# Attention and a squared-ReLU layer on one core: transposes moved from VectorE and TensorE to DMA, with a new order of all engines

## The chip, the cores and the metric

The kernel runs on one core of one Trainium2 chip. Its time is the device time of one execution in microseconds; the time before is 251.46 us, the median of three runs (251.16 to 253.64). The engines of the core run side by side, each through its own queue in order: TensorE (PE in the profile), VectorE (DVE), ScalarE (ACT), GpSimd (POOL) and SyncE (SP). SP only issues DMAs. POOL issues the DMAs that change float32 to bfloat16 under way.

## What is computed

Eight batches of eight heads, 576 tokens, 64 values a head; 32 packing queries a head. Two attentions, then one dense layer with a squared ReLU, on 4608 tokens:

```python
def _attn_ref(q, k, v, p):
    scale = 1.0 / np.sqrt(q.shape[-1])
    def sm_attn(qq, kk, vv):
        s = scale * np.matmul(qq, kk.transpose(0, 1, 3, 2))
        s = s - np.max(s, axis=-1, keepdims=True)
        a = np.exp(s)
        a = a / (np.sum(a, axis=-1, keepdims=True) + 1e-09)
        return np.matmul(a, vv)
    p_packed = sm_attn(p, k, v)
    return sm_attn(q, p_packed, p_packed)

def _moe_ref(x, w_in, w_out):
    r = np.maximum(x @ w_in, 0.0)
    return (r * r) @ w_out
```

`w_in` is 512x2048, `w_out` 2048x512. Inputs and output are float32.

## The kernel before

Work is tiled in quads: four heads of one batch, so two quads a batch, 16 in all. A quad is named by batch and quad, so `s121` is the step `s1` of batch 2, quad 1. The steps of a quad are these.

- `Lk`, `Lq`, `Lv` load keys, queries and values by POOL's queue as bfloat16 (288 KB each), into three buffers for each of the three.
- `kT`, `qT` turn keys and queries in 32x32 blocks on VectorE (lines 279 and 285).
- `s1` (line 295) are the packing queries' scores: 16 TensorE matmuls of 32 rows, 32 columns and 288 moving columns, into PSUM. From batch 2 on both quads run together, with quad 1's heads swapped in pairs (`group`, `PAIRED`), so that eight of these matmuls can lie side by side in the array instead of four.
- `m1`, `x1`, `rd`: row maximum on VectorE, exponential on ScalarE with the sum beside it, reciprocal.
- `eT`, `eo`: six TensorE transposes of the softmax `e1` into PSUM and their copy to SBUF by ScalarE or VectorE.
- `pv` (24 small matmuls) and `pp` (times the reciprocal): the packed values.
- `bd` turns them in 32x32 blocks for the second scores; `pt`, `po` turn them on TensorE and copy them out for `wp`.
- `s2`: scores of the queries, like `s1`; `t2` turns the scores on VectorE (line 383).
- `m2`, `sb`, `x2`, `su`, `a2`, `aT`: the second softmax, and its turn in 32x32 blocks, on VectorE, ScalarE and GpSimd.
- `w0`, `w1` and `W0`, `W1`: the packed values times `w_in` (`wp`, line 422), and copies out of PSUM.

The dense layer follows. `hB.H.F` (`h0.F` in batch 0) makes the hidden block F of batch B, half H: two quads' `wp` times `a2T`, matmuls of 128x128 by 288 columns (line 438). `r` is the ReLU out of PSUM, on ScalarE or VectorE, `q` the square into `gT` on VectorE (line 479). `oT.j` are two of the 16 matmuls of output tile T (line 490), `c` copies the tile out of PSUM and issues its two output DMAs on SP's queue (line 510). There are 36 output tiles and three `o_sb` buffers. `Z` words are idle matmuls on zeros. `Wi`, `Wo`, `Pr`, `P0`, `P1`, `Pt` load and prepare the weights and the packing queries.

Nothing is scheduled by a compiler: the string `ORDER` holds one word for each step, a suffix names the engine (`:v` VectorE, `:a` ScalarE, `:p` GpSimd), and every engine takes its instructions in the order of the words. Waits follow from the tiles that are read and written. An engine whose next instruction waits holds everything behind it.

Of the kernel before, what the change touches and what calls it, by code (L numbers as in the profile page):

```python
# [21 lines left out]
D = 64  # L22
# [9 lines left out]
PAIRED = range(2, 8)  # L32
# [21 lines left out]
o3.5 po20:a bd21 h1.0.12 h1.0.3 w020 q1.0.2 o3.6 r1.0.12:a r1.0.3:a h1.0.7 h1.0.13 q1.0.0 Lk30 qT20 o3.7 W020:a bd20
o4.0 r1.0.13:a c3:a r1.0.7:v q1.0.1 h1.0.10 q1.0.6 h1.0.11 q1.0.3 s22 r1.0.10:a h1.0.8 r1.0.11:a r1.0.8:a h1.0.9
Lq30 o4.1 t220 h1.0.14 r1.0.9:a o4.2 t221 q1.0.4 r1.0.14:a h1.1.0 r1.1.0:a pt21 h1.0.15 m221 o4.3 po21:a h1.1.2
r1.0.15:a w021 w120 q1.0.5 h1.1.10 o5.0 sb21:v r1.1.2:a W021:a o4.4 h1.1.8 m220 x221 Lv31 r1.1.10:a sb20:v o5.1 Lk31
r1.1.8:a x220 o4.5 h1.1.3 r1.1.3:a h1.1.11 o4.6 r1.1.11:a kT30 W120:a h1.1.4 kT31 r1.1.4:a w121 q1.0.7 h1.1.1 o5.2
o4.7 r1.1.1:a h1.1.6 o5.3 su20 W121:a su21 Lq40 h1.1.5 r1.1.5:a r1.1.6:v c4:a o5.4 s13 a221:v h1.1.7 q1.1.0 r1.1.7:a
h1.1.14 q1.1.5 o5.5 r1.1.14:a h1.1.15 r1.1.15:a a220:v Lk40 o5.6 aT21 o5.7 q1.1.1 q1.1.2 h1.1.12 q1.1.3 Lk41 aT20  # L60
c5:a h1.1.13 Lq31 r1.1.12:a o6.0 o6.1 h1.1.9 r1.1.13:a r1.1.9:a o6.2 Lv41 m131 h2.0.2 q1.1.4 r2.0.2:a h2.0.3 o6.3
m130 h2.0.0 r2.0.3:a o6.4 h2.0.4 kT40 q1.1.7 r2.0.0:a x130 o7.0 h2.0.8 r2.0.4:a o6.5 Lv30 r2.0.8:a eT30 x131 h2.0.6
rd30 o7.1 eo30:v h2.0.7 o7.2 eT31 r2.0.6:a q1.1.6 o6.6 o6.7 qT30 r2.0.7:a rd31 qT31 q2.0.1 h2.0.1 h2.0.14 pv30
eo31:a r2.0.1:a pv31 o7.3 pp31:a c6:a r2.0.14:v h2.0.5 q2.0.0 o7.4 h2.0.10 pp30:a r2.0.5:v o7.5 bd30 r2.0.10:a
h2.0.12 pt30 r2.0.12:a o7.6 h2.0.9 h2.0.11 po30:a kT41 w030 bd31 w130 r2.0.11:a W030:a r2.0.9:v q2.0.3 h2.1.6 q2.0.2
r2.1.6:a h2.0.13 o7.7 r2.0.13:a o8.0 W130:v c7:a h2.0.15 h2.1.7 r2.0.15:a s23 q2.0.4 h2.1.0 r2.1.7:v q2.0.7 o8.1
r2.1.0:a h2.1.14 t230 o8.2 t231 h2.1.12 r2.1.14:a Lq41 q2.0.6 m231 o8.3 o8.4 Lv40 r2.1.12:a pt31 q2.0.5 h2.1.1 o8.5
o9.0 h2.1.15 r2.1.1:a h2.1.4 r2.1.4:a o8.6 r2.1.15:a o9.1 o8.7 m230 h2.1.10 po31:v sb31:v o9.2 h2.1.13 x231 o9.3
o9.4 r2.1.10:a sb30:v su31 r2.1.13:a h2.1.8 q2.1.3 c8:a w131 w031 q2.1.0 h2.1.11 o9.5 x230 r2.1.8:v r2.1.11:a a231:v
W031:a q2.1.6 h2.1.2 o9.6 r2.1.2:v h2.1.5 su30 o9.7 a230:v q2.1.7 h2.1.3 aT31 W131:a r2.1.5:a o10.0 o10.1 o10.2 s14  # L70
h2.1.9 aT30 c9:a r2.1.3:a o10.3 q2.1.1 h3.0.8 o10.4 o10.5 r2.1.9:a r3.0.8:a h3.0.2 h3.0.0 m140 q2.1.4 x140 m141
r3.0.2:a x141 q2.1.2 q2.1.5 o11.0 eT40 eo40:v h3.0.6 o11.1 r3.0.0:a rd41 o11.2 h3.0.3 eT41 r3.0.6:a h3.0.1 qT40 qT41
r3.0.3:a o10.6 Lk50 eo41:a r3.0.1:v h3.0.7 o10.7 rd40 q3.0.1 pv40 pv41 r3.0.7:a pp40:v q3.0.0 h3.0.4 h3.0.5 pt40
o11.3 r3.0.4:a h3.0.9 c10:v Lk51 o11.4 r3.0.5:v r3.0.9:a q3.0.4 o11.5 h3.0.10 o11.6 po40:a pp41:a h3.0.12 pt41 bd40
r3.0.10:a q3.0.3 h3.0.14 r3.0.14:v r3.0.12:a o11.7 h3.0.15 bd41 w140 po41:a q3.0.2 w040 r3.0.15:v h3.1.2 W040:a
o12.0 W140:a o12.1 r3.1.2:v h3.0.11 o12.2 o12.3 kT51 q3.0.7 r3.0.11:v h3.1.0 kT50 s24 h3.1.4 r3.1.0:v c11:a o12.4
t241 o12.5 r3.1.4:a o12.6 h3.1.5 o12.7 r3.1.5:a h3.0.13 q3.0.5 r3.0.13:a o13.0 h3.1.6 o13.1 m241 c12:a sb41:v h3.1.3
r3.1.6:a r3.1.3:a x241 t240 o13.2 h3.1.1 r3.1.1:a o13.3 h3.1.7 o13.4 o13.5 r3.1.7:a q3.0.6 Lv51 m240 sb40:v h3.1.8
Lq51 w141 w041 q3.1.2 o13.6 o14.0 r3.1.8:a x240 h3.1.9 su41 o13.7 o14.1 Lv50 h3.1.14 W041:a c13:a a241:v r3.1.9:v
r3.1.14:a h3.1.15 o14.2 su40 W141:a o14.3 q3.1.1 h3.1.12 o14.4 r3.1.15:a s15 aT41 h3.1.10 o14.5 Lv61 a240:v o14.6  # L80
r3.1.12:a q3.1.0 h3.1.13 r3.1.10:a aT40 q3.1.4 m150 m151 h4.0.2 r3.1.13:a o15.0 o15.1 h4.0.10 r4.0.2:a o14.7 q3.1.6
q3.1.3 o15.2 x150 h4.0.4 r4.0.10:a o15.3 h3.1.11 c14:v r4.0.4:v x151 eT50 eo50:a q3.1.7 eT51 h4.0.8 r3.1.11:v q3.1.5
o15.4 h4.0.5 Lk61 r4.0.8:v o15.5 eo51:v h4.0.12 Lk60 r4.0.5:v pv50 pv51 h4.0.9 rd51 r4.0.12:a o16.0 h4.0.11 Lq50
r4.0.9:a q4.0.4 rd50 o16.1 r4.0.11:a pp50:v pp51:a h4.0.3 o16.2 pt51 qT50 o15.6 h4.0.0 po51:v r4.0.3:a r4.0.0:a
q4.0.5 o15.7 Lq60 h4.0.14 pt50 c15:a q4.0.1 h4.0.1 o16.3 r4.0.14:a o16.4 po50:v r4.0.1:v h4.0.15 h4.1.0 w050 q4.0.2
w150 bd51 r4.1.0:a r4.0.15:a o16.5 h4.0.6 kT60 q4.0.0 h4.1.1 r4.1.1:a q4.0.7 o16.6 bd50 r4.0.6:v o17.0 h4.1.2 Lk71
W050:a h4.1.3 r4.1.2:a W150:v o17.1 o17.2 qT51 r4.1.3:a h4.0.13 kT61 r4.0.13:a h4.0.7 q4.0.6 s25 h4.1.6 t251
r4.0.7:a t250 o16.7 q4.1.0 o17.3 o17.4 o17.5 c16:a m250 r4.1.6:a h4.1.10 h4.1.4 r4.1.4:a o17.6 sb50:v w151 w051
r4.1.10:a h4.1.5 h4.1.11 o17.7 m251 o18.0 r4.1.5:a h4.1.8 r4.1.11:a o18.1 Lq71 q4.0.3 qT60 c17:a h4.1.9 Lk70 o18.2
q4.1.2 o18.3 o18.4 o18.5 r4.1.8:a sb51:v W051:a o18.6 o19.0 x250 r4.1.9:a x251 W151:a h4.1.12 h4.1.7 q4.1.1 o18.7  # L90
c18:a o19.1 r4.1.12:a Lq61 su50 s16 a250:v o19.2 su51 a251:v m160 h4.1.14 r4.1.7:a o19.3 h4.1.13 o19.4 aT50
r4.1.14:a x160 o19.5 aT51 q4.1.3 m161 Lv60 h4.1.15 o19.6 r4.1.13:a h5.0.10 o20.0 r4.1.15:a h5.0.2 x161 q4.1.5 q4.1.4
o19.7 r5.0.2:a o20.1 eT61 r5.0.10:v h5.0.6 h5.0.3 eT60 c19:v r5.0.6:a o20.2 r5.0.3:v eo60:a q4.1.6 h5.0.4 eo61:v
r5.0.4:a h5.0.7 o20.3 q5.0.1 rd61 pv60 r5.0.7:a rd60 pp60:v pv61 h5.0.0 q4.1.7 Lv70 h5.0.11 o20.4 pt60 r5.0.0:a
h5.0.1 o20.5 r5.0.11:v pp61:a h5.0.5 o21.0 r5.0.1:a o20.6 po60:a h5.0.8 r5.0.5:a h5.1.2 qT61 kT71 q5.0.5 w160 q5.0.3
bd60 w060 q5.0.2 r5.0.8:a r5.1.2:a W060:a o21.1 h5.0.9 kT70 o21.2 W160:a r5.0.9:v bd61 Lv71 o20.7 o21.3 h5.1.3
q5.0.0 r5.1.3:v h5.0.14 s26 t260 h5.0.15 c20:a r5.0.14:a h5.0.12 r5.0.15:a r5.0.12:a o21.4 h5.1.0 o21.5 r5.1.0:a
q5.1.1 t261 h5.1.12 r5.1.12:a h5.1.1 o22.0 q5.0.4 r5.1.1:a h5.0.13 m260 o22.1 r5.0.13:v o21.6 h5.1.4 pt61 r5.1.4:a
sb60:v po61:a h5.1.13 o21.7 r5.1.13:a h5.1.6 o22.2 m261 q5.0.7 h5.1.14 x260 r5.1.6:a o22.3 r5.1.14:a o22.4 c21:a
sb61:v h5.1.5 h5.1.7 r5.1.5:a r5.1.7:a o22.5 su60 w061 q5.1.6 w161 q5.0.6 h5.1.15 h5.1.8 Lq70 x261 a260:v r5.1.15:a  # L100
q5.1.0 q5.1.2 aT60 o22.6 W061:a o22.7 o23.0 h5.1.10 r5.1.10:v o23.1 o23.2 r5.1.8:a h5.1.11 o23.3 c22:a o23.4 W161:a
su61 h5.1.9 q5.1.3 s17 o23.5 r5.1.11:a o24.0 a261:v aT61 o23.6 m170 h6.0.6 m171 r5.1.9:a o24.1 h6.0.2 o23.7 x170
# [525 lines left out]
```

## Time and profile before

| | |
|---|---|
| median of three runs | 251.46 us (251.16 to 253.64) |
| span of the profiled execution, first to last instruction | 248.6 us (its own time is not given beside the span) |
| first hidden matmul starts | 23.15 us |
| first output matmul starts | 37.28 us |
| last output matmul ends | 243.84 us |
| granted TensorE clock, mean | 0.995 |
| TensorE's share of the chain that ended last | 81% |
| cast loads: 288 KB, issue to landing, median | 7.2 to 8.1 us |
| output DMA: 128 KB, issue to landing, median | 2.8 us |

The span counts from the first to the last instruction of the core. Matmuls are pipelined: the duration of one in the groups is its latency, and what a step costs TensorE is read from the starts in the timeline. The chain of waits is followed back from the last instruction to whatever released it. The DMA share counts packets in flight on 16 engines and can exceed 1.

### The profile page before, as it was taken

To read this page: it belongs to the slowest core of one execution; us is meant where nothing else is said; L and a number is where in the kernel's file an instruction comes from. 1 tells how busy PE (TensorE), PEld (TensorE's weight loads), DVE (VectorE), ACT (ScalarE), POOL (GpSimd) and SP (SyncE) were. 2 spreads that over 40 slices of the span, in tenths; PEclk is the share of its full clock that TensorE was granted. 3 is DMA by queue.
4 is the path that set the end of the run, shared out by engine and by line. 5 is a ranking of instruction groups with operands and counts; after the bars stand their busy time and mean duration, and the time that the engine had idled before them with its cause. 6 is when DMAs were issued, how large, how long until landed. Compare 5 with 4: busy or idle time off the path is not lost.

```text
span 248.6 us, 6041 instructions
## 1 busy us (share of the span) xinstructions
PE 237.1 (95%) x2415; PEld 132.2 (53%) x2447; DVE 194.2 (78%) x411; ACT 145.7 (59%) x316; POOL 45.8 (18%) x75
## 2 busy tenths in 40 slices
PE   8998899998999999999999999999999999999992
PEld 5655554465556554655456555655555555555540
DVE  1888899978988899979887998898897798644710
ACT  2346784476968748755764658676957555353100
POOL 8329634350401500033000230010000000000000
PEclk9999999999999999999999999999999999999997
DMA  6999999999791992269812794252121213211323
GB/s 112 203 207 205 206 197 209 197 142 259 161 171 64 157 211 45 46 93 187 185 42 45 135 130 122 64 90 56 42 45 42 45 42 82 49 42 44 70 63 82
DMA packets 23358, 28.52 MB, mean 115 GB/s; under 512 B 4257, under 2 KB 14753, under 8 KB 23329
## 3 DMA queue, kind: packets, MB, share of 16 engines
q0 software_dynamic: 16880, 18.55, 47.1%
q1 hardware_dynamic: 6288, 9.44, 15.0%
q8 instruction: 19, 0.31, 0.5%
q10 hardware_dynamic: 160, 0.13, 0.2%
q14 instruction: 11, 0.08, 0.1%
HBM read 37.22 MB, written 9.44 MB: 188 GB/s over the span
## 4 chain that ended last, share of the span: by engine, by line
PE 81%; DMA 10%; issue 2%; DVE 2%; POOL 2%; ACT 1%; SPq 0%; ACTq 0%; POOLq 0%
PE ps_o L490 48%; PE ps_h L438 24%; DMA v_b<-in_v_dram 4%; PE ps_wp L422 3%; PE ps_s L295 3%; DMA w_in_bf<-in_moe_w_in_dram 3%; DMA out_dram<-o_sb 3%; PE ps_e1T L339 1%; PE ps_pv L352 1%; POOL k_b L242 1%; DVE mx L387 1%; POOL d L391 0%; ACT r L444 0%; POOL q_b L242 0%; PE ps_ppT L372 0%
## 5 line engine op out<-in xcount | busy, mean ns | idle before, releaser
L490 PE MATMUL ps_o<-w_out_bf,gT 128*128 128x512 bf16 x544 | 144.2, 379 | 2.0 <-issue 0.5
L444 ACT ACTIVATE r<-ps_h 128x288 bf16<-128x288 f32 (+1 forms) x181 | 73.1, 426 | 55.9 <-PE ps_h L438 47.5
L438 PE MATMUL ps_h<-a2T,wp 128*128 128x288 bf16 x512 | 91.9, 286 | 1.4 <-ACT r L444 1.4
L490 PEld LDWEIGHTS <-gT 128*128 128x128 bf16 x576 | 54.9, 98 | 42.1 <-issue 3.3
L438 PEld LDWEIGHTS <-wp 128*128 128x128 bf16 x512 | 47.4, 98 | 44.4 <-issue 7.7
L479 DVE TENSOR_TENSOR gT<-r 128x576 bf16<-128x576 bf16 x128 | 54.7, 448 | 5.2 <-ACT r L444 4.9
L446 DVE TENSOR_SCALAR r<-ps_h 128x288 bf16<-128x288 f32 (+1 forms) x59 | 28.5, 484 | 20.0 <-PE ps_h L438 18.8
L332 ACT CAST wp<-ps_wp 128x1024 bf16<-128x1024 f32 x29 | 28.9, 1016 | 3.8 <-PE ps_wp L422 3.7
L332 ACT COPY o_sb<-ps_o 128x512 f32<-128x512 f32 x27 | 15.9, 588 | 10.8 <-PE ps_o L490 9.4
L321 ACT ACTIVATE e<-ps_s,nm 128x576 bf16<-128x576 f32 x16 | 11.8, 736 | 13.0 <-DVE nm L316 13.0
L233 POOL DMA_DIRECT2D v_b<-in_v_dram x16 | 11.1, 695 | 44.2 <-PE ps_pv L352 22.5
L279 DVE STREAM_TRANSPOSE kT<-k_b 128x576 uint32<-128x576 uint32 x16 | 15.0, 943 | 5.1 <-DMA k_b<-in_k_dram 5.1
L263 PE MATMUL ps_idle<-nought 128*128 128x288 bf16 x95 | 14.4, 304 | 1.1 <-DVE nought L178 1.1
L383 DVE STREAM_TRANSPOSE s<-ps_s 128x576 f32<-128x576 f32 x16 | 12.0, 767 | 2.4 <-PE ps_s L295 2.4
L401 DVE TENSOR_REDUCE sums<-e 128x18 f32<-128x576 f32 x16 | 11.9, 741 | 1.4 <-ACT e L396 1.3
L242 POOL DMA_DIRECT2D k_b<-in_k_dram x16 | 9.0, 562 | 21.4 <-DVE kT L279 12.5
L422 PE MATMUL ps_wp<-w_in_bf,ppT 64*32 64x512 bf16 x256 | 11.4, 382 | 0.8 <-DMA w_in_bf<-in_moe_w_in_dram 0.7
L316 DVE TENSOR_REDUCE nm<-ps_s 128x1 f32<-128x576 f32 x16 | 11.6, 739 | 0.6 <-PE ps_s L295 0.6
L285 DVE STREAM_TRANSPOSE qT<-q_b 128x576 uint32<-128x576 uint32 x16 | 12.0, 761 | 0.0
L387 DVE TENSOR_REDUCE mx<-s 128x18 f32<-128x576 f32 x16 | 11.9, 743 | 0.1
L396 ACT ACTIVATE e<-d 128x576 f32<-128x576 f32 x16 | 11.0, 685 | 1.6 <-DVE d L391 1.4
L263 PEld LDWEIGHTS <-nought 128*128 128x128 bf16 x95 | 9.2, 103 | 4.9 <-issue 1.2
(47 smaller groups left out, 153.0 us busy)
## 6 DMA issues: line engine op xcount, KB each, us to landing
out_dram<-o_sb SPq DMA_DIRECT2D x70, 128.0 KB, 2.8
k_b<-in_k_dram POOLq DMA_DIRECT2D x16, 288.0 KB, 8.1
v_b<-in_v_dram POOLq DMA_DIRECT2D x16, 288.0 KB, 7.4
q_b<-in_q_dram POOLq DMA_DIRECT2D x10, 288.0 KB, 7.2
w_in_bf<-in_moe_w_in_dram POOLq DMA_DIRECT2D x4, 512.0 KB, 12.5
w_out_bf<-in_moe_w_out_dram POOLq DMA_DIRECT2D x4, 512.0 KB, 13.8
q_b<-in_q_dram POOLq DMA_DIRECT2D x12, 144.0 KB, 3.9
p_b<-in_p_dram POOLq DMA_DIRECT2D x1, 192.0 KB, 11.5
```

Of the source, the lines that this page charges most:

```text
L263: self.nc.tensor.matmul(ps[:, :HALF], lhsT=self.nought[:, :P], rhs=self.nought, start=True, stop=True)
L279: return self.nc.vector.transpose(t["kT"][:].rearrange("p (j l a) e -> p a j l e", j=J, a=3).bitcast(U32).rearrange("p a j l e -> p a j (l ...
L285: return self.nc.vector.transpose(t["qT"][:].rearrange("p s e -> p (s e)").bitcast(U32), t["q"][:].rearrange("p t d -> p (t d)").bitcast(U32))
L332: engine.copy(out, x)
L383: nc.vector.transpose(s2[:].rearrange("p (a t) i -> p a (t i)", a=2), t["ps_s2"][:, :, :HALF])
L387: self.nc.vector.tensor_reduce(out=t["mx"], in_=t["s2"], op=ALU.max, axis=AX.X)
L422: self.nc.tensor.matmul(ps[NP * h:NP * h + NP, c, :], lhsT=t["ppT"][D * c:D * c + D, NP * g:NP * g + NP], rhs=self.w_in_bf[D * c:D * c + D ...
L438: self.nc.tensor.matmul(ps, lhsT=t["wp"][:, fb // n, fb % n * P:(fb % n + 1) * P], rhs=t["a2T"][:, hf * HALF:(hf + 1) * HALF], start=(qd = ...
L444: engine.activation(r, ps, ACT.Relu)
L446: engine.tensor_scalar_max(r, ps, 0.0)
L479: (engine or self.nc.vector).tensor_tensor(out=out, in0=r, in1=r, op=ALU.mult)
L490: self.nc.tensor.matmul(self.o[tt], lhsT=self.gT[:, fb, a:a + P], rhs=self.w_out_bf[:, fb, :], start=(i == 0), stop=(i == self.NFB - 1))
```

## The change

- From batch 2 on, `kT`, `qT`, `eT`, `pt` are single DMA transposes, issued on SP's queue: 9 blocks of 128x128 for keys, 9 for queries, 6 for `e1`, one for the packed values. A sixth word, `Px`, turns a batch's packing queries (two blocks). The copies `eo` and `po` of these batches are gone.
- In batches 0 and 1 keys and queries are turned by nine TensorE transposes each (`kP`, `qP`) into PSUM and copied out (`kE`, `qE`); `eT` and `pt` stay on TensorE.
- A turned tile now has the 64 values of a head on 64 partitions, even and odd tokens in the two halves, so `s1` is 8 matmuls of 64 rows (from 16 of 32 rows), and so is `s2` from batch 2 on. In batches 0 and 1 `s2` is 72 matmuls of 32 moving columns that give the scores already turned; these have no `t2`. `bd`, `group` and `PAIRED` are gone.
- The keys of batch 0 are loaded as float32 on SP's queue, into space of `gT`, and cast by ScalarE and VectorE (`ka`, `kb`). The packing queries come on ScalarE's queue.
- `e1` lies in two fixed tiles with padded columns that are zeroed at the start.
- `c` is split: the copy stays `c`, the two output DMAs become a word `d`.
- Squares name an engine: 79 on VectorE, 49 on GpSimd. ReLUs are 131 on ScalarE and 109 on VectorE (181 and 59 before); output copies 14 and 21, besides the last tile's (27 and 8 before); subtractions on GpSimd 7 (3 before), multiplications 6 (3).
- All words stand in a new order; there are 59 idle matmuls for 95.

The core of the diff, with the order of the start and of batch 2's and the start of batch 3's attention:

```diff
-PAIRED = range(2, 8)
+TURNED = range(2, 8)
...
+Lk00 I Lk01 Lv01 Lq01 Pd:v Lq00 PT Lv00 PE:v kb00:a ka00:v Wi01 Z9 kP00 Wi00 kb01:v ka01:a Lk11 kE00:a Z5 kP01 Wi11
+kE01:v s100 Wi10 m100 Z2 s101 m101 x100 Lk10 x101 Z9 eT00 rd00 qP01 eo00:v eT01 rd01 Lq10 qE01:a qP00 eo01:v qE00:v
+pv01 pp01:a pv00 Wo2 pt01 pp00:v po01:a pt00 s201 po00:v s200 m201 m200 Lv11 sb01:v sb00:v x201 x200 su01 Z22 w000 Wo0
+w001 W000:a su00 a201:p W001:a a200:v Z6 kP11 Lv10 aT01 kE11:a aT00 Z6 h0.1 h0.11 r0.1:v Pr s111 r0.11:a m111 h0.10
...
+r1.0.4:v o5.0 r1.1.11:a o4.1 rd20 h1.0.5 eT20 h1.1.10 r1.0.5:v o5.1 r1.1.10:a h1.1.4 q1.0.2:v q1.1.5:p h1.1.3 kT31
+r1.1.4:v o4.2 r1.1.3:a pv21 q1.1.1:v Lq41 h1.0.13 pp21:a h1.0.12 r1.0.13:v o5.2 Px4 Lv30 r1.0.12:a h1.1.8 pt21
+q1.0.6:v h1.0.14 r1.1.8:a r1.0.14:v h1.0.6 pv20 r1.0.6:v h1.0.7 pp20:a Lv41 h1.1.9 r1.0.7:v pt20 s221 r1.1.9:a w021
+q1.0.3:v h1.0.15 q1.1.4:p W021:a t221 h1.1.5 kT30 o5.3 r1.1.5:v o4.3 r1.0.15:a m221 Lk40 w121 s220 q1.0.7:p q1.1.2:v
...
-        self.sm = pool("sm", 2)
+        self.sm = pool("sm", 4)
...
+        nc.scalar.dma_start(self.p_f, self.packed(0, G))
...
+        self.e1s = [self.consts.tile([P, J, P], BF16, name=f"e1x{i}") for i in range(2)]
+        for x in self.e1s:
+            nc.vector.memset(x[:, :, PS:], 0.0)
...
+    def p_x(self, b):
+        self.pX[b] = self.tp.tile([P, self.NQ, P], BF16, name="pX")
+        g = (b - TURNED[0]) * self.NQ
+        self.nc.sync.dma_start_transpose(self.pX[b], self.p_d[:, g:g + self.NQ].rearrange("p g e d -> p (g e d)"))
...
+            if (n, b) == ("k", 0):
+
+                f = self.gT[:, self.NFB - 1 - qd, :].bitcast(F32).rearrange("p (t d) -> p t d", d=D)
+                self.nc.sync.dma_start(f, s)
+                self.att.setdefault((b, qd), {})["f"] = f
...
+    def st_turned(self, t, n):
+        x = t[n + "T"] = self.tp.tile([P, T // 2, P], BF16, name=n + "T")
+        self.nc.sync.dma_start_transpose(x, t[n][:].rearrange("p t d -> p (t d)"))
...
+    def st_turn(self, t, n):
+        ps = t["ps_" + n] = self.turn16("ps_" + n)[:].rearrange("p a c -> p (a c)")[:, :T * D]
+        x = t[n][:].rearrange("p t d -> p (t d)")
+        for i in range(T // 2):
+            self.nc.tensor.transpose(ps[:, i * P:(i + 1) * P], x[:, i * P:(i + 1) * P], self.ident)
+
+    def st_turn_out(self, t, n, engine):
+        t[n + "T"] = self.tp.tile([P, T // 2, P], BF16, name=n + "T")
+        self.copy(engine, t[n + "T"][:].rearrange("p t c -> p (t c)"), t["ps_" + n])
+
+    def st_s1(self, t, b, qd):
+
+        ps = t["ps_s1"] = self.turn32("ps_s1")
+        for h in range(QH):
+            c = slice(NP * h, NP * h + NP)
             for e in range(2):
...
+                r = slice(D * e, D * e + D)
+                self.nc.tensor.matmul(ps[c, e, :HALF].rearrange("p (b a l) -> p a b l", a=3, b=3),
+                                      lhsT=self.pX[b][r, qd, c],
+                                      rhs=t["kT"][r, :, c].rearrange("p (a b) l -> p a b l", a=3), start=True, stop=True)
...
+        if b in TURNED:
+            for h in range(QH):
+                c = slice(NP * h, NP * h + NP)
+                for e in range(2):
+                    r = slice(D * e, D * e + D)
+                    self.nc.tensor.matmul(ps[c, e, :HALF], lhsT=t["ppT"][r, c], rhs=t["qT"][r, :, c], start=True, stop=True)
+            return
+
+        for i in range(T // 2):
+            for e in range(2):
+                for h in range(QH):
+                    r, c = slice(D * e, D * e + D), slice(NP * h, NP * h + NP)
+                    self.nc.tensor.matmul(ps[c, e, i * NP:(i + 1) * NP], lhsT=t["qT"][r, i, c], rhs=t["ppT"][r, c],
+                                          start=True, stop=True)
...
     def st_e1T(self, t, b):
+        if b in TURNED:
+            t["e1T"] = self.tp.tile([P, J, P], BF16, name="e1T")
+            self.nc.sync.dma_start_transpose(t["e1T"], t["e1"][:].rearrange("p j s -> p (j s)"))
+            return
...
     def st_ppT(self, t, b):
+        if b in TURNED:
+            t["ppT"] = self.keep.tile([P, P], BF16, name="ppT")
+            self.nc.sync.dma_start_transpose(t["ppT"][:].unsqueeze(1), t["pp"][:].rearrange("p e d -> p (e d)"))
+            return
...
+    def step_d(self, engine, tt):
+        nc, o = self.nc, self.o_sb.pop(tt)
```

## The prediction

> **What bounds the kernel now.** I read the busy table and the forty slices first, then the stages, then the costliest groups, then the landing times of the queue that the change loads.
>
> ```profile
> PE 237.1 (95%) x2415; PEld 132.2 (53%) x2447; DVE 194.2 (78%) x411; ACT 145.7 (59%) x316; POOL 45.8 (18%) x75
> ...
> DMA  6999999999791992269812794252121213211323
> ```
>
> TensorE is busy in nearly the whole span, and the DMA engines are full for the first quarter and half empty later. The stages (busy us of PE, PEld, DVE, ACT, POOL, then clock, DMA share, GB/s) say where an engine other than TensorE can matter:
>
> ```profile
> 0.00:23.10 23.10, 20.51 (x275) 13.06 (x275) 15.30 (x31) 9.76 (x16) 12.82 (x23) 1.00 1.07 180
> 23.10:37.30 14.20, 12.96 (x188) 7.81 (x185) 12.11 (x27) 10.83 (x18) 7.99 (x13) 1.00 1.34 202
> 37.30:60.00 22.70, 21.64 (x244) 10.91 (x245) 20.47 (x41) 12.69 (x26) 8.21 (x12) 1.00 1.13 199
> 60.00:120.00 60.00, 59.37 (x618) 33.34 (x627) 52.77 (x112) 43.17 (x100) 11.59 (x20) 1.00 0.71 133
> 120.00:180.00 60.00, 59.37 (x622) 32.89 (x630) 52.05 (x111) 40.92 (x93) 5.24 (x9) 1.00 0.46 87
> ```
>
> From 60 us on TensorE idles 1%, with VectorE at 87%: work taken off VectorE there gains little by itself, work taken off TensorE counts in full. The timeline gives the price of each TensorE step, start to start, where the groups give single latencies only:
>
> ```profile
> 51.53 0.83 PE L339 MATMUL ps_e1T<-ident,e 128*96 128x128 bf16 x12
> 52.20 0.59 PE L490 MATMUL ps_o<-w_out_bf,gT 128*128 128x512 bf16 x2
> 52.63 0.65 PE L438 MATMUL ps_h<-a2T,wp 128*128 128x288 bf16 x4
> 53.21 0.56 PE L352 MATMUL ps_pv<-v_b,e1T 96*32 96x64 bf16 x48
> 53.70 0.67 PE L438 MATMUL ps_h<-a2T,wp 128*128 128x288 bf16 x4
> ```
>
> So 12 transposes of `e1` take 0.67 us (0.335 a quad, 56 ns each), two output matmuls 0.43 (0.216 each), two pv steps 0.49. The same view gives 4 hidden matmuls 0.49 (0.122 each), a wp step alone 0.35 and two together 0.56: 0.216 a step (8 matmuls at once) and 0.13 for each run of small tiles among full ones. Likewise 0.62 for a score step alone (33.18 to 33.80; 4 at once) and for a pair (57.99; 8 at once): 4 x 0.122 + 0.13. A ppT transpose takes 0.06.
>
> From the first hidden matmul (23.15 us) to the end of the last output matmul (243.84) are 220.7 us. Work in it: 576 output matmuls 124.2, 512 hidden 62.6; batches 2 to 7 at 1.23 scores + 0.67 eT + 0.12 pt + 0.34 pv + 0.86 wp + some three further change-overs = 3.64 each, 21.8; batch 1 by the same prices 3.4, batch 0's last wp 0.7. Sum 212.8 (rounded), so 7.9 us are stalls. Before 23.15 lies a chain of loads and single small steps, with 95 idle matmuls as filler. Behind the last matmul lie 4.8 us, whose code stays the same.
>
> **TensorE's work, part by part.** In batches 2 to 7 the score steps become 8 matmuls of 64 rows, all on different parts of the array as in wp: 0.122 a quad and 0.13 where the run is new. Four score steps cost 0.49 for 0.98 of columns, but stand mostly alone, as wp now does too. eT (0.67) and pt (0.12) leave TensorE. Counted through the order with these prices a batch costs 2.45 instead of 3.64; six batches gain 7.1 us.
>
> Batch 1 pays: one kP and two qP of 9 transposes (0.5 each), two s1 and one more eT that now stand behind the first hidden matmul, and two s2 of 72 matmuls of 32 columns for 0.62 each before. The trace has no such form; pv's 48 in 0.49 (10 ns each) give 0.7, the paired scores' 32 in 0.62 (19 ns) 1.4. I take 1.1, the middle. Batch 1 comes to 6.9 for 3.4. The stretch holds 124.2 + 62.6 + 14.7 + 6.9 + 0.7 = 209.1: 3.7 us less.
>
> **The start.** `k00` and `k01` come as floats on SP's queue, 576 KB written each where a cast load wrote 288, beside POOL's four loads. Best case: issue at 0.74 and 2.2 to landing as `p_f`, plus 1152 KB at the page's best slice (259 GB/s): 7.3 us. Worst: half of the 207 GB/s: 12.4. I take 9.5 for `k01`: `k00` largely alone, as POOL's loads begin after the identity, `k01` at half rate. Then casts, 9 transposes and an eviction of 128x1152 from PSUM (1.0 by the 128x1024 cast): 2.4 to the scores; from there max 0.76, exp 0.74, transposes and eviction 1.0, pv, pp, pt, po 1.2, two s2 2.2, semaphores 0.6: 6.5; then the order fills Z22, two wp, Z6, kP11, Z6, 5.2 us, about the length of max, subtract, exp, sums, multiply and turn. First hidden matmul: 9.5 + 2.4 + 6.5 + 5.2 = 23.6, half a microsecond later than now (21.4 to 26.5 by the bounds). The idle matmuls, `I`, `Pd`, PT and the zeroing of the padding lie under these loads at no cost; without that cover they are 1 to 2 us. `w_in` comes by the same POOL queue behind one load less and is not last.
>
> **VectorE, ScalarE, GpSimd.** VectorE loses 15.0 (kT), 12.0 (qT), 3.1 (ppd), four turns of scores 3.1, 49 squares 20.9, and some 9 of subtracts, multiplies and evictions; it takes 50 more ReLUs (22.7), 13 output copies (9.0), five wp copies (6.1), three evictions (2.3): 171 for 194. ScalarE falls to about 107. GpSimd takes 49 squares; nearest row is its 128x576 multiply, 1.16 us (lower bound VectorE's 0.43), so 57 us, and seven more element-wise steps 8: 111 us of work. A square that lands late holds only the output matmuls that read that block; loads queue behind it on POOL. In this order a load of `v` stands 0.5 to 1.5 us of TensorE work behind the pv step that frees its buffer. I set these at no cost while the six `r` buffers cover a square, and take 2 of the 7.9 us of stalls off for the freer VectorE and ScalarE, since 2.3 us of TensorE's idle time lies between 23.1 and 60 where VectorE is at 85 to 90% (bounds 0 and 4).
>
> **SP's queue.** It carries, for a batch, 18 + 18 + 12 + 2 + 2 blocks of 128x128 (keys, queries, softmaxes, ppT, p), 312 in all, 10.2 MB, among the output DMAs (0.59 us issue each, two a tile). An instruction there that waits holds the transposes and output DMAs behind it; with three `o_sb` buffers, output copies wait only after three tiles. No row shows a transpose by DMA. The nearest are output DMAs of 128 KB:
>
> ```profile
> DMA to landing us min/median/max: 7.2/7.4/7.6
> ```
> ```profile
> DMA to landing us min/median/max: 2.3/2.4/2.5
> ```
>
> The first is those issued from 50 to 53 us, while loads run, the second those from 200 to 210. The final 64 KB pieces take 2.0. The order leaves 5.5 us or more of TensorE work from kT or qT to its scores, 3.5 to 23 from eT to pv: covered in quiet stretches. The tight place is pt: from pp's step to s2 the order holds, by quad from 20 to 71, 2.4, 2.2, 4.3, 2.6, 3.3, 2.5, 3.4, 4.8, 3.9, 8.3, 2.0 and 4.6 us. Needed are pp 0.37, 0.1 of semaphores and the landing X. TensorE is in order, so hidden and output matmuls behind s2 wait too. Summing the shortfalls (a pair stalls once): X = 2.2 costs 1.5 us, 2.8 costs 3.9, 4.5 costs 15. ppT has 32 KB; I take 2.2, between the 64 KB and quiet 128 KB rows.
>
> Against this part speaks a rule: the Trainium skill, "VectorE: DVE Perf Modes", section on the three transpose paths, gives 390 ns for a 128x128 bf16 transpose on TensorE and 1309 ns by DMA, and advises TensorE where PSUM will do. By it 312 blocks one after another are 408 us (an estimate from that page), and the kernel would take far longer; no run here shows either figure for DMA. The skill's "DMA: Bandwidth & Descriptors", latency section, has 261 GB/s for one kernel's DMA transposes, 39 us by the same kind of estimate, and then the queue holds.
>
> **Sum.** First hidden matmul 23.6 + work 209.1 + stalls 7.9 - 2.0 + 1.5 = 7.4, + 4.8 behind = 244.9 us of span, against 248.6. The execution's own time is not given beyond its span; taking the 2.9 us between span and median (251.46) as fixed, 247.8 us.
>
> **Rivals.** (C) Slower: the turned ppT lands late because loads and larger transposes share the DMA engines. For it: landings of 7 us at 50 to 60 and again of 6.8 at 80 to 90; against: 2.3 to 3.4 at 90 to 100, and ppT's small size. With X = 7 for batches 2 and 3 the first pt of each costs 5.3 and 4.9, the rest at 2.7 costs 1.8: 12 us in place of 1.5, about 258 us. It decides from X = 3.0 (no gain) and is over 1% slower from 3.4.
>
> (D) SP issues a transpose block by block. At the output DMA's 0.59 us each, 312 blocks are 185 us, with 25 tiles' outputs 215, in the 158 or so in which they must pass: 57 us more, about 305. For it: two-part outputs do cost twice; against: one instruction per tile.
>
> (E) GpSimd is late: if each square and descriptor job takes 1.5 times 1.16, it has 140 us of work, and loads queue behind; half a microsecond of stall for each square from batch 2 on (some 40) gives 268. For it: POOL waited up to 21.8 us for one buffer; against: it was 18% busy.
>
> (F) Larger gain: keys land at 7.3 and 4 us of stalls go: 243.6.
>
> **Chances.** Forecast (247.8, own range 243.5 to 250.5) 0.48, C 0.37, D 0.04, E 0.04, F 0.07. Over 1% is about what a measurement here can tell: below 248.9 lie 0.39 of the forecast's and F, 0.46; within 1% 0.09 and 0.03 of C, 0.12; the rest slower, 0.42. The range 242 to 260 leaves out D, most of E and the upper third of C, under 0.2.
>
> **What would show it.** Right: about 7.1 us less TensorE work in batches 2 to 7, score steps of 8 matmuls at 0.12 and 0.13, the first hidden matmul near 24, ppT landing by 2.4, TensorE idle under 2% from 60 us. Wrong: waits of `ps_s` for the ppT transpose, or of `ps_pv` for `e1T`, of several microseconds; output DMAs queued behind transposes; POOL busy throughout; `ps_o` waiting for squares.

## The result, and the profile after

The changed kernel takes 311.44 us, the median of four runs (309.0 to 316.25), against 252.29 us for four runs of the kernel before: 1.232 times as long, 95% interval 1.222 to 1.242. The profiled execution is the longest of the four (316.25 us, span 314.3). The forecast was 247.8 us in a range of 242 to 260: wrong in sign, and far outside.

The page of the changed kernel, first its busy times, the granted clock in forty slices, the packets of the DMA queue on which SP issues, and the chain that ended last:

```profile
PE 254.0 (81%) x2403; PEld 131.8 (42%) x2403; DVE 196.4 (63%) x368; ACT 125.3 (40%) x238; POOL 109.1 (35%) x123
...
PEclk9989999966776998796998995999799999999999
...
q1 hardware_dynamic: 47712, 20.72, 38.0%
...
PE 46%; DMA 26%; DVE 18%; ACT 5%; issue 2%; SPq 1%; DVEq 0%
```

Before, 81% of that chain was TensorE and 10% DMA; now it is 46% and 26%, and TensorE's share of the span falls from 95 to 81%. No other engine has become the bound: VectorE has gone from 78 to 63%, ScalarE from 59 to 40%, GpSimd from 18 to 35%. The time is waiting. TensorE's waits name what it waited for (total, times, longest). The longest line of that list before, then four lines of it after:

```profile
PE ps_h L438 <- ACT r L444: 1.4, 3, 0.9
```
```profile
PE ps_s L320 <- DMA ppT<-pp: 23.7, 6, 6.4
PE ps_s L309 <- DMA kT<-k_b: 7.8, 1, 7.8
PE ps_pv L373 <- DMA e1T<-e1x: 5.7, 2, 4.7
...
PE ps_wp L440 <- DMA ppT<-pp: 3.3, 2, 2.6
```

Together 40.5 us for turned tiles, 27.0 of them for the packed values `ppT`. The stages show where, and that the clock goes with it (columns as in the stages of before):

```profile
60.00:80.00 20.00, 11.82 (x69) 5.59 (x66) 8.02 (x17) 5.79 (x13) 6.38 (x7) 0.74 1.28 132
80.00:100.00 20.00, 9.25 (x105) 4.06 (x106) 5.66 (x11) 3.33 (x8) 5.48 (x7) 0.66 1.35 157
```

In these forty microseconds TensorE is idle for 18.9 and every other engine for more, and the granted clock is 0.74 and 0.66; in the stages of before it was 1.00. The timeline shows what that does to a step (start, duration, step, then the idle time before it):

```profile
142.39 0.44 PE L320 MATMUL ps_s<-qT,ppT 64*32 64x288 bf16 x8 [5.01 <-DMA ppT<-pp]
142.77 1.14 PE L456 MATMUL ps_h<-a2T,wp 128*128 128x288 bf16 x4
143.70 1.06 PE L508 MATMUL ps_o<-w_out_bf,gT 128*128 128x512 bf16 x2
144.55 0.69 PE L456 MATMUL ps_h<-a2T,wp 128*128 128x288 bf16 x2
```

After a wait of 5.01 us, four hidden matmuls take 0.93 us from start to start (0.49 before) and two output matmuls 0.85 (0.43): twice the price, at a granted clock of 0.50 in this stretch (142.4 to 145.0).

The account of the 65.7 us between the two spans (314.3 and 248.6):

| stretch | before | after | more |
|---|---|---|---|
| to the first hidden matmul | 23.15 | 28.58 | 5.4 |
| from there to the end of the last output matmul: TensorE idle, as the timeline marks it | 2.6 | 45.4 | 42.8 |
| same stretch: its steps, start to start less that idle time | 218.1 | 235.5 | 17.4 |
| behind the last output matmul | 4.8 | 4.8 | 0.0 |

The 17.4 us belong to a kernel that was to have 3.7 us less work there, so some 21 us went into steps that took longer.

### The profile page after: what moved, and what is told of

It is laid out like the page before. It is cut to its first block, busy times and chain, and to the rows that moved or that the text cites. A ratio compares the mean times of both kernels' runs of the same rounds, so it can differ in the third digit from the quotient of the medians.

```text
span 314.3 us, 6074 instructions
## 1 busy us (share of the span) xinstructions
PE 254.0 (81%) x2403; PEld 131.8 (42%) x2403; DVE 196.4 (63%) x368; ACT 125.3 (40%) x238; POOL 109.1 (35%) x123
## 3 DMA queue, kind: packets, MB, share of 16 engines
q1 hardware_dynamic: 47712, 20.72, 38.0%
HBM read 37.22 MB, written 9.44 MB: 148 GB/s over the span
## 4 chain that ended last, share of the span: by engine, by line
PE 46%; DMA 26%; DVE 18%; ACT 5%; issue 2%; SPq 1%; DVEq 0%
PE ps_o L508 25%; DMA ppT<-pp 14%; PE ps_h L456 11%; DMA kT<-k_b 6%; DMA e1T<-e1x 4%; DVE gT L497 4%; DVE r L464 3%; PE ps_idle L271 3%; PE ps_wp L440 2%; ACT e1x L338 2%; DVE a L426 2%; DVE nm L333 2%; DVE sums L420 2%; DMA p_f<-in_p_dram 1%; PE ps_s L320 1%
## 5 line engine op out<-in xcount | busy, mean ns | idle before, releaser
L508 PE MATMUL ps_o<-w_out_bf,gT 128*128 128x512 bf16 x576 | 161.7, 395 | 1.1 <-ACT r L462 1.0
L456 PE MATMUL ps_h<-a2T,wp 128*128 128x288 bf16 x512 | 99.8, 301 | 4.1 <-DVE r L464 2.0
L497 POOL TENSOR_TENSOR gT<-r 128x576 bf16<-128x576 bf16 x49 | 57.9, 1183 | 110.2 <-ACT r L462 68.4
L462 ACT ACTIVATE r<-ps_h 128x288 bf16<-128x288 f32 (+1 forms) x131 | 54.3, 428 | 76.2 <-PE ps_h L456 74.1
L464 DVE TENSOR_SCALAR r<-ps_h 128x288 bf16<-128x288 f32 (+1 forms) x109 | 50.9, 471 | 30.8 <-PE ps_h L456 28.3
L497 DVE TENSOR_TENSOR gT<-r 128x576 bf16<-128x576 bf16 x79 | 46.5, 591 | 7.3 <-ACT r L462 5.5
L338 ACT ACTIVATE e1x<-ps_s,nm 128x576 bf16<-128x576 f32 x16 | 19.4, 1229 | 12.2 <-DVE nm L333 12.0
L350 DVE COPY o_sb<-ps_o 128x512 f32<-128x512 f32 x21 | 14.5, 691 | 13.3 <-PE ps_o L508 12.9
L348 ACT COPY o_sb<-ps_o 128x512 f32<-128x512 f32 x14 | 8.2, 585 | 13.7 <-PE ps_o L508 13.6
L426 POOL TENSOR_TENSOR a<-e,rs 128x576 bf16<-128x576 f32 x6 | 7.2, 1194 | 18.2 <-DVE rs L422 18.2
L320 PEld LDWEIGHTS <-ppT 64*32 64x32 bf16 x96 | 1.4, 93 | 27.3 <-DMA ppT<-pp 25.8
## 6 DMA issues: line engine op xcount, KB each, us to landing
w_out_bf<-in_moe_w_out_dram POOLq DMA_DIRECT2D x4, 512.0 KB, 12.6
```

What stands on the lines that cost most here:

```text
L338: self.nc.scalar.activation(e1[:, :, :PS].rearrange("p (e b) (l a) -> p e b a l", e=2, a=3), t["ps_s1"][:, :, :HALF].rearrange("p e (b a l ...
L348: engine.copy(out, x)
L350: engine.tensor_copy(out, x)
L426: engine.tensor_tensor(out=t["a2"][:].rearrange("p t i e -> p t e i"), in0=t["e2"][:].rearrange("p (t e) i -> p t e i", e=2), in1=t["rs"][ ...
L456: self.nc.tensor.matmul(ps, lhsT=t["wp"][:, fb // n, fb % n * P:(fb % n + 1) * P], rhs=t["a2T"][:, hf * HALF:(hf + 1) * HALF], start=(qd = ...
L462: engine.activation(r, ps, ACT.Relu)
```

## The experiments

The theories: (A) transposes by DMA are quick by themselves and land late while the loads run; (B) they are slow or costly to issue whatever runs beside them (rival D of the prediction is its strong form); (C) the new order, or ReLUs and evictions on other engines, hold TensorE and would do so without any DMA; (E) GpSimd's squares; (H) a wait costs a second time, because TensorE's clock falls. A time given without its range is a single run; the four runs of the changed kernel lie 7 us apart, so small differences of single runs tell nothing.

**The transposes by themselves.** A kernel that computes nothing of the reference issues transposes of one, six and nine blocks and plain copies of the same bytes, one at a time, first with nothing beside them, then beside cast loads, then beside output stores.

```diff
+sets("quiet", 4)
...
+for i in range(44):
+    y = ld.tile([P, T * D], BF16, name="y")
+    nc.gpsimd.dma_start(y, rows(i % 8, i // 8 % 2))
...
+sets("load", 4)
...
+for i in range(30):
+    nc.scalar.dma_start(out[i * P:(i + 1) * P, :], o)
+sets("store", 3)
```

> Transposes by DMA by themselves: one, six and nine blocks of 128x128, each waited for, then the same beside cast loads, then beside output stores; also plain copies of the same bytes, and one block issued right behind nine. The kernel computes none of the reference. Theory A (they are quick by themselves and slow when they share the DMA engines with loads): one block 2.3 to 2.8 us alone, nine blocks 3.0 to 3.5; beside cast loads nine blocks 6 us or more and one block 3 to 4. Theory B (a transpose is slow by itself, by the block): nine blocks 6 us or more even alone, and eight of nine blocks in a row 5 us or more each.

The instructions of two tiles of this kernel, one block each, quiet and beside loads (duration of the issue, then issue to landing):

```profile
L35 SPq DMA_TRANSPOSE quietone<-x x4: 1120/1122/1186, 5.1 to 45.2; - x4
...
DMA to landing us min/median/max: 2.2/2.2/2.3
```
```profile
L35 SPq DMA_TRANSPOSE loadone<-x x4: 1118/1121/1122, 86.0 to 177.9; - x4
...
DMA to landing us min/median/max: 2.2/5.3/5.6
```

One block lands in 2.2 us when quiet, just the value that the prediction took; six in 2.7, nine in 3.2, a copy of nine blocks' bytes in 2.4. One block issued right behind nine lands in 2.4, and eight transposes of nine blocks in a row in 3.4 each. Beside cast loads one block takes 5.3 (3 to 4 were expected), six 6.6, nine 6.2 (the 2.2 is one issued when the loads had ended), and a copy suffers alike (3.7 for one block's bytes against 1.7 quiet, 6.0 for nine). Beside stores alone one takes 3.0 and nine 4.7. Waited for one at a time, a transpose holds SP at its issue for 1.1 to 1.3 us whatever its size. So A holds; B and the issue block by block (D) fall. The Trainium skill, "Advanced Engine Details and Errata", section on the X-bar transpose, says that transposes on this chip are as fast as ordinary DMAs: the measurement differs, as quiet transposes took 1.3 times as long as copies of the same bytes.

**Packed values turned by TensorE.** `ppT` of batches 2 to 7 goes back to TensorE, with its copy out of PSUM by ScalarE; two of the twelve (`pt31`, `pt40`) also stand later in the order.

```diff
-        if b in TURNED:
-            t["ppT"] = self.keep.tile([P, P], BF16, name="ppT")
-            self.nc.sync.dma_start_transpose(t["ppT"][:].unsqueeze(1), t["pp"][:].rearrange("p e d -> p (e d)"))
-            return
...
-pt21
+pt21 po21:a
```

> The changed kernel with ppT of batches 2 to 7 turned by TensorE and copied by ScalarE, all else as it is. If the late ppT is the main wait (theory A with ppT as the place), the 27 us of TensorE waits for it go, and some 10 to 15 us of half clock with them: 265 to 280 us. If keys and softmaxes only take its place as the last to land, 285 to 300. If GpSimd's squares or ScalarE's exponential hold the kernel (theory C), 300 or more.

286.86 us: 24.6 less, for 12 of 54 transposes, which is the branch in which other transposes take the place of `ppT`. TensorE's largest waits are now these:

```profile
PE ps_s L310 <- DMA kT<-k_b: 9.1, 3, 5.9
PE ps_p L223 <- DVE p L218: 5.3, 1, 5.3
PE ps_h L453 <- DVE r L461: 4.8, 5, 2.4
PE ps_o L505 <- POOL gT L494: 3.1, 2, 2.4
```

Keys step into the place of the packed values, with 9.1 us for 7.8 in the changed kernel: TensorE now reaches them sooner. The 5.3 us on `ps_p` lie at the start. GpSimd's squares appear too, with 3.1 us.

**No loads.** Batches 2 to 7 compute on the keys, queries and values of batch 1, which are not loaded again; the transposes stay.

```diff
     def load1(self, b, qd, n):
+        if b > 1:
+            self.att.setdefault((b, qd), {})[n] = self.att[1, qd][n]
+            return
```

> The changed kernel without the loads of keys, queries and values of batches 2 to 7 (it uses batch 1's in their place), all transposes by DMA as they are. Theory A (the loads make the transposes late): ppT lands in 2.7 to 3.5 us and the time falls to 252 to 268 us. Theory B (transposes slow by themselves): landings stay above 5 us and the time above 295. Theory C: above 290 with quick landings.

274.61 us, 36.8 less, 6.6 us above the range that A gave. The tile `ppT` in this kernel, and the waits:

```profile
DMA to landing us min/median/max: 2.3/2.3/4.2
```
```profile
PE ps_s L323 <- DMA ppT<-pp: 6.0, 5, 2.2
...
PE ps_wp L443 <- DMA ppT<-pp: 2.1, 2, 1.4
```

With all other transposes in place but no loads, the packed values land in 2.3 us where the changed kernel had a median of 6.5 (2.7 to 9.1). Even then 8.1 us of waiting is left, where the prediction had 1.5 for a landing of 2.2. A part of it is SP's queue. The end of a `pp` on VectorE (start, duration), and what SP issued after it:

```profile
96.94 0.35 DVE L385 TENSOR_SCALAR pp<-ps_pv,rden 128x128 bf16<-128x128 f32 x1 [0.23 <-PE ps_pv L376]
```
```profile
97.42 1.77 SPq L358 DMA_TRANSPOSE e1T<-e1x  x1
99.28 1.20 SPq L537 DMA_DIRECT2D out_dram<-o_sb  x2
100.53 1.24 SPq L390 DMA_TRANSPOSE ppT<-pp  x1
```

This `pp` is done at 97.29 and its transpose is issued at 100.53, behind another transpose and two output DMAs; four of the twelve were issued 1.3 to 3.2 us late in this way, in the changed kernel four by 1.5 to 2.4. The prediction had 0.1 us for semaphores and nothing for what stands ahead in that queue. How the 8.1 us divide between this, the order's slack and one landing of 4.2 us, no run shows.

**Nothing turned by DMA.** All four kinds of batches 2 to 7 go to TensorE, with copies out by ScalarE, at places of the order where one of the two `psa` buffers is free.

```diff
-kT20
+kP20 kE20:a
...
-qT20
+qP20 qE20:a
...
-eT21
+eT21 eo21:a
...
-pt21
+pt21 po21:a
```

> The changed kernel with keys, queries, softmaxes and ppT of batches 2 to 7 all turned by TensorE (50 transposes a batch, about 2.9 us of TensorE's time a batch, 17 in all) and copied by ScalarE; only p is still turned by DMA. Theories A and B: 258 to 272 us, with TensorE idle under 5% from 60 us on. Theory C: above 285.

292.88 us, with a clock of 0.993, on the side of C (above 285) by what was expected, not of A (258 to 272). The waits for transposes are gone, but TensorE's steps between the first hidden and the last output matmul take 240.2 us (235.5 after, 218.1 before): the 18 transposes for each quad's keys and queries are real work, and 17.5 us of idle time remain, 7.5 of them on ScalarE's ReLUs, which stand behind the added copies. The added TensorE work and copies cause much of this, so the run does not tell how much belongs to the order by itself.

**All squares on VectorE.**

```diff
-q1.0.5:p
+q1.0.5:v
...
```

> All 49 squares of GpSimd move to VectorE; nothing else changes. If the time is set by transposes that land late (A): GpSimd's lateness is not on the path, VectorE gets 49 x 0.45 = 22 us more work and has room: 305 to 317 us, near the changed kernel's 311.4. If GpSimd's late squares hold the output matmuls, or its work holds the loads on its queue (E): below 302 us. VectorE's own squares should fall from 591 ns to the 448 ns of the kernel before, as GpSimd works less beside it.

308.13 us (304.07 to 308.59), 1.217 times before (1.209 to 1.226), which overlaps with the changed kernel's 1.222 to 1.242: at most a few microseconds. TensorE still waits 33.0 us for transposes. E is not the cause. VectorE's squares take 469 ns here (448 were expected), against 591 with GpSimd's squares beside them.

**No loads, and packed values on TensorE.** The two edits together.

```diff
+        if b > 1:
+            self.att.setdefault((b, qd), {})[n] = self.att[1, qd][n]
+            return
...
-pt21
+pt21 po21:a
```

> Without the loads of keys, queries and values of batches 2 to 7 (batch 1's stand in their place) and with the packed values of all batches turned by TensorE. If late transposes are all that is left beside the start (A): the run without loads, 274.6 us, still waited 8.1 us for the packed values and worked some 7 us at half clock; without them 262 to 267 us. If order and the other engines (ReLUs, the evictions added here) take their place (C): 269 to 277 us.

265.53 us (265.0 to 265.91), as A had it. Two of the longest waits, behind 5.8 us for the first matmul of all, and the clock:

```profile
PE ps_h L456 <- DVE r L464: 3.4, 6, 1.1
PE ps_s L331 <- issue: 2.5, 1, 2.5
```
```profile
PEclk9997999999999999999999999999999999999999
```

No transpose is waited for, and behind the start the clock holds. Of the 59 us that the change cost, 46 went with the loads and with the transposes of the packed values. 13.2 us above the kernel before are left (14.8 between the spans, 263.4 and 248.6): 5.2 at the start (where the 2.5 us of the second line lie), 6.3 of other idle time (8.9 against 2.6; ReLUs of VectorE 3.4 and of ScalarE 2.1, the rest softmaxes and others below 1.2 each), and 3.5 in TensorE's steps (221.6 against 218.1). What C can claim lies within these 13 us.

**The same with all squares on VectorE.**

```diff
-q1.0.5:p
+q1.0.5:v
...
```

> As the kernel before in this list (no loads of batches 2 to 7, packed values turned by TensorE), with all squares on VectorE. If GpSimd's squares were a cause of the rest (E): at least 3 us less than that kernel. If not (A, C): within 2 us of it, or up to 4 us more, since VectorE gets 22 us of work.

266.81 us (266.26 to 268.48), against 265.53: E falls here too.

**The clock held.** Idle matmuls on zeros into unused columns of the tile that waits, in front of seven of the longest waits. They do not shorten a wait; they only keep TensorE busy during it.

```diff
+    FILL = {("s1", 2, 1): 60, ("s2", 2, 1): 52, ("s2", 3, 1): 40, ("s2", 4, 1): 40, ("s2", 5, 0): 34, ("s2", 6, 0): 18,
+            ("pv", 2, 1): 38}
+    def fill(self, ps, *x):
+        for _ in range(self.FILL.get(x, 0)):
+            self.nc.tensor.matmul(ps, lhsT=self.nought[:, :P], rhs=self.nought[:, :224], start=True, stop=True)
```

> The changed kernel with idle matmuls (224 columns, on zeros, into unused columns of the waiting tile) in front of the seven steps where TensorE waited longest: 60, 52, 40, 40, 34, 18 and 38 of them, each less than the wait. If a wait costs a second time because TensorE then works at half clock (H): the waits stay, the half clock of some 51 us after the first hidden matmul falls below 20, and the time falls by 8 to 15 us to 296 to 303. If the landings alone set the time (each wait grows by what the faster work gains), or the clock falls for another reason: 307 to 316 us.

300.15 us (299.12 to 302.4): 11.3 less for 282 matmuls more. The ratio to before is 1.191 (1.184 to 1.197), clear of the changed kernel's.

```profile
PEclk9987999999999999999979999999999999999999
```

The mean granted clock is 0.981 for 0.913 in the profiled executions (0.981 to 0.987 and 0.910 to 0.933 over the four runs of each); over the spans that is 5.7 us of clock lost for 27.3. Idle time and filling together stay at 43 us (16.4 us idle and 282 x 0.095), as the 45.4 us of waits were, and the other steps of TensorE fall from 235.5 us to 222.9. H holds: the landings set the waits, and the half clock cost some 11 us on top. The Trainium skill, "TensorE: Matmul & The Clock Gate", section on the clock gate, gives the rule that TensorE drops to half rate after an idle window of about 3.4 us; here, in the changed kernel, the clock was halved in pieces of 3.4 to 10.2 us that began in or up to 1.3 us behind waits of 2.4 to 7.8 us, so waits below 3.4 us sufficed too (2.44, 2.48 and 2.60).

**First keys by cast loads.** The float loads and the four casts are taken back.

```diff
-            if (n, b) == ("k", 0):
+            if False:
...
-kb00:a ka00:v
...
-kb01:v ka01:a
```

> One part undone: the keys of batch 0 come as cast loads on GpSimd's queue, as in the kernel before, and the four casts are gone; TensorE still turns them. The kernel before had its first scores at 7.05 us with such loads, the changed one at 11.02. If the float load and the cast are what makes the start late: first scores at 8 to 9.5 us, first hidden matmul 1.5 to 3 us earlier than the 28.58 of the changed kernel, 306 to 311 us in all. If the other loads of that queue (288 KB each, now two more) are late instead: first scores earlier, but first hidden matmul at 28 to 30 us, and no gain.

311.71 us (309.34 to 315.4), no gain: first scores at 10.71 us (11.02), first hidden matmul at 28.92 (28.58). Neither branch held in full: the first scores came hardly sooner, since the second tile of keys now landed later (TensorE waited 1.03 us for it) and stands ahead of them in the order. In the time as a whole the way of loading the first keys makes no difference that shows.

**Fewer idle matmuls early.** `Z9` and `Z5` in front of the first turns are taken out, and also the `Z9` in front of the first `eT`, which the expectation does not count: 23 idle matmuls in all.

```diff
-Wi01 Z9 kP00
+Wi01 kP00
...
-kE00:a Z5 kP01
+kE00:a kP01
...
-x101 Z9 eT00
+x101 eT00
```

> The changed kernel without the two early runs of 9 and 5 idle matmuls. TensorE stopped for 2.4 us after 80 of the 144 score matmuls of batch 0's queries, with an instruction packet of DMA under way. If TensorE's queue of instructions had run dry there (I): the stop falls 10 to 14 matmuls later, after some 94 of 144, and stays about as long. If it stops for data or a semaphore: it stays after 80. Time 309 to 317 us; TensorE's clock may be halved earlier.

311.52 us. Batch 0's query scores in the changed kernel and in this one:

```profile
17.57 0.78 PE L327 MATMUL ps_s<-ppT,qT 64*32 64x32 bf16 x80
20.79 0.67 PE L327 MATMUL ps_s<-ppT,qT 64*32 64x32 bf16 x64 [2.44 <-issue]
21.39 4.26 PE L271 MATMUL ps_idle<-nought 128*128 128x288 bf16 x22
```
```profile
16.72 0.97 PE L327 MATMUL ps_s<-ppT,qT 64*32 64x32 bf16 x103
21.32 0.50 PE L327 MATMUL ps_s<-ppT,qT 64*32 64x32 bf16 x41 [3.63 <-issue]
21.75 4.87 PE L271 MATMUL ps_idle<-nought 128*128 128x288 bf16 x22
```

TensorE started these scores 0.85 us earlier, stopped after 103 instead of 80 and went on at about the same time, 21 us. With 23 idle matmuls fewer ahead of it, the stop came exactly 23 score matmuls later: in both kernels it stands behind TensorE's 223rd matmul and 224th weight load, and so it does in every other kernel here that has these small score matmuls. It is tied to the number of instructions, not to data. In both kernels one packet of the instruction queue starts between 18 and 19 us; that TensorE waits for instructions is the reading that fits, but the profile has no row for their supply. Then 22 idle matmuls cost 4.2 us in place of 2.7, at half clock.

**Eight matmuls for a quad's query scores** in batches 0 and 1 too, turned by VectorE as in the kernel before.

```diff
-        for i in range(T // 2):
...
-                    self.nc.tensor.matmul(ps[c, e, i * NP:(i + 1) * NP], lhsT=t["qT"][r, i, c], rhs=t["ppT"][r, c],
+                self.nc.tensor.matmul(ps[c, e, :HALF], lhsT=t["ppT"][r, c], rhs=t["qT"][r, :, c], start=True, stop=True)
...
-s201 po00:v s200 m201 m200
+s201 po00:v s200 t201 m201 t200 m200
```

> The changed kernel with the queries' scores of batches 0 and 1 as 8 matmuls of 288 columns, turned by VectorE (0.78 us each) as in the later batches, in place of 72 small ones that need no turn: 64 matmuls and their weight loads less for a quad. If TensorE's instructions run dry in batch 0's small matmuls (I): the stop of 2.4 to 3.6 us there goes or moves behind the idle matmuls, TensorE does not fall to half clock for it, and the first hidden matmul comes at 24.5 to 27 us in place of 28.58, in spite of 1.6 us of turns. If the stop is set by the time at which one packet of instructions lands, whatever the count: it is met by the next steps, and the first hidden matmul stays at 28 to 29.5 us. The whole time, 306 to 314 us, tells little.

```profile
17.34 0.49 PE L319 MATMUL ps_s<-qT,ppT 64*32 64x288 bf16 x16
17.76 2.87 PE L271 MATMUL ps_idle<-nought 128*128 128x288 bf16 x22
```

No stop, and the idle matmuls run at full clock. The first hidden matmul comes at 26.36 us, 2.2 sooner, although two turns by VectorE stand in the chain. The whole took 304.0 us in its one run; the rest of that difference lies within what the waits vary by (31.5 us for transposes here).

**Keys and queries on TensorE, the rest by DMA.** All loads run; the transposes of nine blocks are gone from SP's queue, and their steps stand at the places of the run with nothing turned by DMA.

```diff
-kT20
+kP20 kE20:a
...
-qT20
+qP20 qE20:a
```

> Keys and queries of batches 2 to 7 are turned by TensorE and copied out by ScalarE; only e1 and the packed values are still turned by DMA, and all loads run. TensorE gets some 12 us of work and the copies. If loads make the transposes late (A): the packed values still land 5 to 8 us after issue while loads run, and the waits for them stay at 15 us or more. If the large transposes of keys and queries ahead of them did it (C of the prediction's two causes): landings of 2.5 to 3.5 us, waits below 6 us. Time 285 to 305 us by the one, 270 to 282 by the other.

309.05 us, above the 285 to 305 that A gave. The packed values that were issued between 70 and 210 us, while loads run:

```profile
L388 SPq DMA_TRANSPOSE ppT<-pp x9: 1108/1126/1358, 76.2 to 209.3; - x9
...
DMA to landing us min/median/max: 4.3/5.6/7.8
```

In the changed kernel the median between 85 and 220 us is 6.9. So they are late without the larger transposes too, as A had it (5 to 8 us); those may add about one microsecond. TensorE still waits 16.2 us for packed values (A: 15 or more), and its steps between the first hidden and the last output matmul take 240.4 us for 235.5.

Contention shows in the DMA queues themselves. Between 60 and 100 us (packets, MB, and the time for which packets were in flight as a share of 16 engines), before and after:

```profile
q0 software_dynamic: 2955, 3.82, 59.0%
q1 hardware_dynamic: 1014, 1.65, 13.1%
```
```profile
q1 hardware_dynamic: 10115, 3.38, 78.5%
q0 software_dynamic: 1671, 2.36, 52.1%
```

Twice the bytes on SP's queue come in ten times the packets, which are in flight for six times the share; the loads beside them, on `q0`, have a share of 22% for a megabyte where they had 15%. The Trainium skill, "DMA: Bandwidth & Descriptors", section on queues and completion order, has each engine change between queues packet by packet; that fits, but no run here shows the change itself.

No kernel of this study comes below the 252 us of the kernel before.

## Why the prediction was wrong

- **TensorE's attention work: right; its steps as a whole: not.** Summed start to start, the attention steps behind the first hidden matmul took 27.6 us before and 23.2 in the run without loads, 4.4 less (forecast 3.7 less). The 72 small score matmuls of a quad took 0.66 us (48.82 to 49.48), not 1.1. But even in the run without late transposes all steps of that stretch took 3.5 us more than before, so the hidden and output matmuls took some 8 us more there, a term that the sum did not have.
- **The failed step: the landing of `ppT`.** "I take 2.2, between the 64 KB and quiet 128 KB rows" chose the quiet row for a transfer that is issued while loads run, though the fence above it showed the same queue at 7.4 us beside loads. It measured 2.7 to 9.1, median 6.5. The 1.5 us of stalls that hung on it became 27.0 us of waits. The prediction's own sums held the warning: a landing of 4.5 was to cost 15 us (some 13 by the twelve slacks as printed, a pair counted once). The same slacks give some 25 us for a landing of 6.5, near the 27.0; that is partly luck, since at the 2.3 us of the run without loads they give below 2 and the run waited 8.1. Nothing was put either for the time that a transpose of `ppT` stands behind others in SP's queue (0.03 to 2.4 us from the end of `pp` to the issue).
- **This step is not all.** Without the loads and with `ppT` on TensorE the kernel still took 265.53 us, above the forecast and above the kernel before: the start, the stalls that were to shrink and the longer steps cost it those 13 us.
- **"Covered in quiet stretches": wrong for the same reason.** Keys landed up to 17.7 us after issue (6.6 median) and cost 7.8; `e1T` landed up to 10.0 and cost 5.7. The cover of 5.5 us was priced against quiet landings only.
- **No term for the clock.** A wait was priced at its length. Beyond the 45.4 us of idle time TensorE's steps grew by 17.4 us; filling seven of the waits took 11.3 us off the time, the mean clock rose from 0.913 to 0.981, and the steps fell by 12.6 us.
- **The start: the sum held up to the scores, then not.** Keys landed by 7.6 us (1.2 + 6.4), sooner than the 9.5 taken, but idle matmuls, turn and copy took the gain, and the second scores began at 11.93, as 9.5 + 2.4 gives. From there 6.5 + 5.2 us became 16.7: the stop of 2.44 us in the small score matmuls and 22 idle matmuls at half clock, 1.6. Both go when those scores are 8 matmuls. Worked like the best bound for the keys, the worst would have been some 14 us and not 12.4; no run came near it.
- **VectorE and ScalarE: too low, GpSimd right.** VectorE was busy for 196.4 us where 171 were forecast, ScalarE for 125.3 where 107 were, GpSimd for 109.1 where 111 were. The squares on VectorE took 591 ns for 448 (79 x 0.143 = 11 us more), and the first exponentials 1229 ns for 736, now written in steps into the padded tile; neither was in the account. That VectorE's squares slow down beside GpSimd's, the runs show (469 ns with none there). VectorE is still only 63% busy. The 2 us of stalls that were to go did not: without late transposes TensorE's idle time behind the first hidden matmul is 8.9 us, where the kernel before has 2.6.
- **Rivals.** C had the mechanism and an X of 7, about the median that came, but gave it to batches 2 and 3 only and without the clock, hence 258. Loads run until 222 us, so it held for batches 2 to 6. D fell as it was put: by itself an issue takes 1.1 to 1.3 us for one block and for nine. But in the changed kernel single issues held SP for up to 6.7 us (medians by tile 1.2 to 2.0), and that queue was not free of cost. E fell (266.81 against 265.53). F fell: nothing was gained. The Trainium skill's advice in "VectorE: DVE Perf Modes", section of rules for kernel authors, to turn on TensorE where PSUM will do, held for `ppT`, which the chain needs at once (24.6 us); for all four kinds it gained less (292.88 us). The Trainium skill's price of 1309 ns a block, one after another, did not show: nine blocks landed in 3.2 us.

What stays open: the 6.3 us of other idle time of the run without late transposes (pieces of up to 1.1 us), and the 8 us or so more of its hidden and output matmuls, which the timeline does not mark as idle and no run separates; and how much of ScalarE's longer exponential matters, which was not tried.

## What to carry to other kernels

Price a transfer that the in-order engine needs at once by its landing beside the traffic that will run with it, not by the quiet row; add what stands ahead of it in the issuing queue; and compare each slack with the worst landing of that stretch. A small tile at the end of a dependent chain is the first to keep on the engine. A TensorE wait of some microseconds costs more than its length: count the half clock behind it, or fill it with idle matmuls.

## What the hardware showed that I had not expected

- The granted clock fell to 0.5 around single waits, from 2.4 us on: in all 27 us of clock lost in a span of 314.3, 6 after filling.
- A DMA transpose by itself kept SP 1.1 to 1.3 us at the issue, one block or nine; a plain copy of the nine blocks' bytes 0.46. In the changed kernel it was up to 6.7 us.
- The transposes' queue carried 47712 packets in 20.72 MB, 434 bytes each on average, before the change 6288 in 9.44.
- TensorE stopped for 2.4 to 3.6 us among 144 score matmuls of 32 columns (9 ns each, with their weight loads), always behind its 223rd matmul, and not at all with 16 matmuls in their place. It fits that it ran out of instructions; the supply itself is in no row.
